# Gated state-space mix: sums of frequency products by accumulating transfers, product scratch by plane, unit matrix made on GpSimd, one new instruction order

## The chip, the core and the metric

The kernel runs on one core of a Trainium2 chip. The metric is the device time of one execution in microseconds (us), as the median of the runs shown. A profiled execution has a time of its own, and a span, which runs from its first instruction to its last.

## What is computed

There are L = 2048 tokens of D = 512 channels in bf16, x = A_u. Cut to what matters:

```python
K = einsum("dn,dnl,dn->dl", C, exp(dt*A*l), dt*B).real   # 128 complex states per channel, l = 0..2047
a = causal_convolution(x, K) + x * Dskip                 # the reference does it with FFTs of 4096
r = x @ w_r;  idx = the two tokens with the largest r
b = x;  b[idx] += (silu(x[idx] @ w_gate) * (x[idx] @ w_up)) @ w_down * sigmoid(r[idx])
g = sigmoid((x * gate_w).sum(-1))
out = g * a + (1 - g) * b
```

## The kernel before, in words

The 2048 tokens are two blocks of 1024 (`m` for inputs, `j` for outputs), and the 512 channels two halves of 256 (`c`, called `hf` in the early parts). The parts in the order of the program text:

- **Lead-in.** The tables of the state matrices are turned by matrix products with a unit matrix (`nt0`, `nt1`, L572), which VectorE (DVE) then combines with `dt`. The unit matrix and its negative (`CI`, 128x256) come by a transfer named `cia` from a constant (L525), which ScalarE (ACT) issues behind the transfer of `log_dt`. GpSimd (POOL) only fills a matrix of ones (`one`, L532). TensorE (PE) runs warm-up products `hm` on the ones (L535) until the data are there.
- **`transform(m)`**: the forward transform of a block, PE products (L870) evacuated by ACT or DVE (`fwo`, `fwe`), then DVE sums `v0`, `v1`, `w0`, `w1`. Two sums of each block are made by a transfer that adds its source into its destination (`vb`, `accum_op`, 512 KB, issued by POOL, L881 and L883).
- **Powers of the states**: exponentials on ACT (L437), DVE products `cm`, `mw`, `mf`, and for each half `coarse` and `fine` (PE phase sums at L681 and L686, sines on ACT, DVE products `pi`, `pr`, `qm`).
- **`lags(c)`**: PE sums over the states (`kmm`, L923), evacuations `kae`, a PE rearrangement `sel` (L937), evacuations `kce`, `kcx`. **`spectrum(c)`**: PE products `ks` (L962) and `kf` (L967), evacuated as `khe`, `khf`: the kernel's spectrum of this half.
- **`products(c, j)`** (L988): products of the token spectra with the kernel's. For j = 0 there are two DVE products (`prod`, 4096 wide), for j = 1 four for each half of the frequencies (2048 wide; `HALVES`, two stages `s_`). They then have to be summed: near block plus far block (j = 1 only), real parts (`yr`: first minus second), imaginary parts (`yi`: first plus second), and then sums and differences of the two frequency groups `hc` (`pq`), and for three of the four (c, j) another level (`b0`, `b2`, `b13`).
- **`inverse(c, j)`** (L1080): for each residue r of four, PE products with the inverse matrix (L1114), plus the residual `(1-g)/g * b` by a scaled unit matrix (L1109; `rd` makes that matrix), plus a correction (L1111), evacuated with the factor g (`ive`; ACT L1125 in two instructions, DVE L1129 in one), and sent out (`out`).
- **`rows`**: the gates, the choice of the two tokens and their feed-forward net: many tiny instructions on all engines, in the middle of the rest.

The product scratch lies in region TP. A product `k` has, for each frequency tile, 256 real and 256 imaginary columns in turn; `yr`, `yi` read runs of 256 columns (`pl_`, L1010). Before, the sums are made in one of two ways, chosen by `SUMPE` (L229): on DVE (`acc`, `yr`, `yi`, `pq`; used for (0, 0), (1, 0) and the first stage of (0, 1)), or on PE, which adds the products in PSUM with the unit matrix and its negative (`ac`, L1030, L1032, L1034), evacuated twice (`ace`) and followed by one `pq` (used for the second stage of (0, 1) and both stages of (1, 1)).

What sets the order: the program text only makes a list of operations with their buffers. `PLAN` (L180) is a written-out order of all of them, with a number for each that picks one of the engines that the operation may run on. Each engine runs its own operations in just that order, and waits with semaphores for what an operation needs (`replay` L128, `emit_plan` L152), also where the earlier operation ran on the same engine (PE excepted). SP, ACT and POOL issue transfers in that order too: a transfer that waits holds everything behind it on its issuing engine. `BANKS` (L215) gives the PSUM banks.

Nearly all DVE work is recorded at the lines of helpers: L408 (`tensor_tensor`), L434 (evacuations), L706 (`ns`), L859 (`fwo`), L1129 (`ive`), L1159 (`rd`); ACT's at L428 (copies and evacuations) and L437 (functions).

Of the kernel before, what the change touches and what calls it, by code (L numbers as in the profile page):

```python
# [179 lines left out]
PLAN = [(0, 0), (4, 0), (5, 0), (6, 0), (7, 0), (8, 0), (9, 0), (10, 0), (11, 0), (12, 0), (13, 0), (14, 0), (3, 0), (27, 0), (1, 1), (48, 0),  # L180
# [45 lines left out]
T2 = NEAR + [258, 262, 260, 264] + [516, 520, 772, 776] + [1032, 1544, 1288, 1800]  # L226
NT2 = 20
NG = 4
SUMPE = {(0, 0): False, (0, 1): (False, True), (1, 0): False, (1, 1): True}  # L229
QUARTER = {(0, 0): True, (0, 1): True, (1, 0): True, (1, 1): False}  # L230
MAGIC = 1.5 * 2.0 ** 39
TURN = 65536.0 / (2.0 * math.pi)
# [1008 lines left out]
```

## Time and profile before

| | |
|---|---|
| runs shown | 147.87, 149.94, 150.06 us; median 149.94 us |
| the profiled execution's own time | 148.18 us |
| its span | 146.4 us, mean granted TensorE clock 0.987 |
| busy | DVE 135.5 us (93%), PE 128.3 (88%), ACT 114.5 (78%), POOL 18.1 (12%) |
| transfers | 26.46 MB, mean 181 GB/s |

How to read it: times count from the start of the span. A group of instructions has its count behind "x", then the time that at least one of them was busy, then the mean of one in nanoseconds, then the idle time ahead of them with what ended it. Instructions of DVE start a little before the one ahead of them has ended, so the busy time of a group divided by its count is less than the mean of one. The chain that ended last is followed back from the last instruction. A line can be a helper's, and stand for many parts of the kernel.

### The profile page before, as it was taken

The numbers are of one execution on the slowest core, as the hardware profiler recorded it, in microseconds if no ns is written. First come the engines' busy times: TensorE is split into PE (matmuls) and PEld (weight loads), VectorE is DVE, ScalarE is ACT, GpSimd is POOL, SyncE is SP. The second block draws the span as 40 slices with busy tenths as digits, with TensorE's granted clock in tenths as the row PEclk, the third lists the DMA queues.
The fourth block names the chain that finished last, engine by engine and source line by source line (L and its number), as shares of the span: only waits on it lengthen the run. The fifth ranks groups of instructions, "written<-read, shape, count | busy, mean of one in ns | idle before, by whom it ended". The sixth has DMA issues, their size and how long they took to land.

```text
span 146.4 us, 3151 instructions
## 1 busy us (share of the span) xinstructions
PE 128.3 (88%) x1302; PEld 89.0 (61%) x1309; DVE 135.5 (93%) x174; ACT 114.5 (78%) x162; POOL 18.1 (12%) x30
## 2 busy tenths in 40 slices
PE   7956719999999979999979998888999898999992
PEld 3842306654434656566735886865888676778881
DVE  0699999989999999999999999999999999999962
ACT  3699999799999989699957878998499734517731
POOL 2000000180304804145310000000000000000000
PEclk9999999689999999999999999999999999999999
DMA  4779999899970809989646693735380050001345
GB/s 135 248 242 236 278 271 258 317 356 321 297 169 0 143 6 318 468 311 285 129 145 177 148 425 158 203 72 222 21 288 0 0 146 4 0 0 40 107 138 150
DMA packets 23741, 26.46 MB, mean 181 GB/s; under 512 B 9224, under 2 KB 20112, under 8 KB 23568
## 3 DMA queue, kind: packets, MB, share of 16 engines
q1 hardware_dynamic: 21134, 23.46, 52.4%
q0 software_dynamic: 1088, 2.10, 7.9%
q10 hardware_dynamic: 1506, 0.72, 1.7%
q8 instruction: 10, 0.16, 0.5%
q14 instruction: 3, 0.02, 0.0%
HBM read 19.85 MB, written 4.20 MB: 164 GB/s over the span
## 4 chain that ended last, share of the span: by engine, by line
DVE 44%; PE 33%; ACT 18%; issue 3%; POOL 0%; DVEq 0%; POOLq 0%
DVE RB L408 36%; ACT RB L437 11%; PE psm L1114 10%; ACT RB L428 6%; PE psm L962 5%; PE psm L1030 4%; DVE RB L434 3%; PE psm L1109 2%; PE psm L937 2%; PE psm L1034 2%; PE psm L1032 2%; DVE RB L706 2%; PE psm L535 2%; PE psm L681 1%; ACT L1186 1%
## 5 line engine op out<-in xcount | busy, mean ns | idle before, releaser
L408 DVE TENSOR_TENSOR RB<-RB 128x2048 bf16<-128x2048 bf16 (+8 forms) x120 | 113.0, 987 | 1.4 <-ACT RB L437 0.2
L428 ACT ACTIVATE RB<-psm 128x1024 bf16<-128x1024 f32 (+7 forms) x44 | 38.1, 898 | 15.4 <-PE psm L1034 9.2
L437 ACT ACTIVATE RB<-psm 128x1024 bf16<-128x1024 int16 (+1 forms) x37 | 36.5, 1033 | 6.4 <-PE psm L686 2.8
L1114 PE MATMUL psm<-RB 128*128 128x256 bf16 x160 | 22.3, 273 | 0.0
L681 PE MATMUL psm<-RB 128*128 128x256 f16 (+1 forms) x112 | 21.1, 336 | 0.2 <-ACT RB L428 0.2
L870 PE MATMUL psm<-RB 128*128 128x512 bf16 x61 | 15.0, 383 | 5.8 <-ACT RB L428 3.8
L437 ACT ACTIVATE RB<-RB 128x512 bf16<-128x512 f32 (+5 forms) x32 | 16.7, 591 | 1.3 <-DVE RB L408 1.2
L1114 PEld LDWEIGHTS psm<-RB 128*128 128x128 bf16 x160 | 15.7, 98 | 1.8
L686 PE MATMUL psm<-RB 128*128 128x512 f16 x44 | 13.5, 393 | 2.8 <-ACT RB L437 2.8
L962 PE MATMUL psm<-RB 128*128 128x256 bf16 x128 | 15.1, 273 | 0.8 <-ACT RB L428 0.8
L681 PEld LDWEIGHTS psm<-RB 128*128 128x128 f16 x112 | 10.8, 101 | 8.0 <-issue 0.5
L870 PEld LDWEIGHTS psm<-RB 128*128 128x128 bf16 x64 | 6.0, 100 | 14.5 <-ACT RB L428 4.7
L962 PEld LDWEIGHTS psm<-RB 128*128 128x128 bf16 x128 | 12.3, 98 | 3.4 <-ACT RB L428 1.6
L1125 ACT ACTIVATE RB<-psm,RB 128x256 bf16<-128x256 f32 x25 | 10.2, 472 | 5.2 <-PE psm L1114 4.2
L923 PE MATMUL psm<-RB 128*128 128x80 bf16 x256 | 10.4, 198 | 0.5 <-ACT RB L428 0.4
L923 PEld LDWEIGHTS psm<-RB 128*128 128x128 bf16 x256 | 9.7, 96 | 1.7 <-ACT RB L428 1.0
L1109 PE MATMUL psm<-RB 128*128 128x256 bf16 x32 | 8.7, 273 | 0.6 <-DVE RB L408 0.4
L428 ACT ACTIVATE RB<-psm,RB 128x1024 bf16<-128x1024 f32 (+1 forms) x9 | 9.2, 1062 | 0.0
L686 PEld LDWEIGHTS psm<-RB 128*128 128x128 f16 x44 | 3.5, 100 | 6.7 <-ACT RB L437 5.9
L1030 PE MATMUL psm<-RB 128*128 128x512 bf16 x21 | 6.5, 380 | 0.8 <-ACT RB L428 0.6
L883 POOL DMA_DIRECT2D RB<-RB x2 | 2.6, 1321 | 32.6 <-ACT RB L428 32.6
L434 DVE CAST RB<-psm 128x1024 bf16<-128x1024 f32 (+3 forms) x6 | 6.4, 1062 | 0.0
(71 smaller groups left out, 119.7 us busy)
## 6 DMA issues: line engine op xcount, KB each, us to landing
RB<-in_A_u_dram SPq DMA_DIRECT2D x8, 256.0 KB, 4.4
RB<-RB POOLq DMA_DIRECT2D x4, 512.0 KB, 9.8
RB<-c_near SPq DMA_DIRECT2D x4, 512.0 KB, 6.5
RB<-c_inv SPq DMA_DIRECT2D x1, 2048.0 KB, 10.4
RB<-u_routed SPq DMA_DIRECT2D x2, 1024.0 KB, 5.4
RB<-in_B_w_gate_dram SPq DMA_DIRECT2D x1, 1792.0 KB, 9.4
RB<-in_B_w_up_dram SPq DMA_DIRECT2D x1, 1792.0 KB, 16.8
RB<-in_B_w_down_dram SPq DMA_DIRECT2D x1, 1792.0 KB, 7.5
```

The lines of the kernel that those rows point to most:

```text
L408: return P.add(name, [(eng, c_dve(n, mode) if eng == DVE else 1.0, lambda h: h.tensor_tensor(out=o(), in0=a_(), in1=b_(), op=op))], rd, wr ...
L428: return lambda h: h.activation(out=o(), in_=a_(), func=ACTF.Copy, scale=scale() if callable(scale) else scale)
L434: return P.add(name, [(ACT, c_act(n), f_act(o, a_)), (DVE, c_dve(n, 1), lambda h: h.tensor_copy(o(), a_()))], rd, wr, **kw)
L437: return P.add(name, [(ACT, cost or c_act(n), lambda h: h.activation(out=o(), in_=a_(), func=func, scale=scale))], rd, wr, table=table, **kw)
L681: r = h.matmul(P32(t, 0, 0, 128, 256 * l0, (1, 256 * nl)), DGM(0, 128, (DD.index(d) + 2) * 128, (1, 128)), src(0, 128, col + hf * CW, (0, ...
L686: r = h.matmul(P32(t, b, 0, 128, 0, (1, 512)), DGM(0, 128, 0, (1, 128)), DGM(0, 128, 128 + c_, (0, 512)), start=False, stop=False, skip_gr ...
L870: x = h.matmul(P32(t, b, 0, 128, 0, (1, 512)), FM(0, 128, 2048 * par + 1024 * pl + 512 * i + 256 * q + 128 * b, (1, 128)), U(0, 128, ((m * ...
L923: x = h.matmul(P32(t, q // 6, 0, 128, (q % 6) * 80, (1, 80)), TPv(0, 128, ri * 16384 + c * 8192 + r * 128, (1, 128)), TQv(0, 128, c * 1024 ...
L962: x = h.matmul(P32(t, kt // 2, 0, 128, (kt % 2) * 256, (1, 256)), KN(0, 128, 2048 * KNP[2 * pl + hc] + 512 * g + 128 * kt, (1, 128)), KC[c ...
L1030: r = h.matmul(P32(t, kt, 0, 128, 0, (1, 512)), CI(0, 128, 0, (1, 128)), f(k, 0, 512), start=(k == 0 and hc == 1), stop=False, skip_group_ ...
L1109: h.matmul(o, RD(0, 128, (tb + 8) % 16 * 128, (1, 128)), UE[q](0, 128, r * 256, (1, 256)) if early else U2(0, 128, tb * D + c * CW, (1, 25 ...
L1114: x = h.matmul(o, G(0, 128, (pl * 4 + kt) * 1024 + (r * 2 + q) * 128, (1, 128)), PQ(0, 128, r * 1024 + kt * 256 + pl * 256 if quarter else ...
```

## The change

1. **Unit matrix.** The transfer `cia` goes. POOL makes `one`, then clears `CI` (`id0`) and writes the diagonals 1 and -1 with two `affine_select` over 128x128 each (`id1`, `id2`).
2. **Summing for c = 0.** `SUMPE` no longer names the second stage of (0, 1): its two `ac` on PE, two `ace` on ACT and one `pq` go, and it gets `yr` and two `pq` on DVE. In both stages of (0, 1) the two `acc` of DVE become one accumulating transfer `acd` of 1 MB that adds near and far products (all four planes). In (0, 0), both stages of (0, 1), and (1, 0) the `yi` of DVE becomes an accumulating transfer `yid` (512, 256, 256 and 512 KB). All six are issued by POOL. `yid` of a stage reads what `acd` of that stage has written.
3. **Planes.** A product summed by DVE or by transfer has all real columns first and then all imaginary ones (the write of `prod` and the reads of `pq` are stepped, `yr` reads whole runs). The second stage of (0, 1) gets scratch of its own (offset 16384 of TP, the first half of the second half-channel powers that `kmm` of `lags(1)` reads). The second stage of (1, 1) gets the region of the near matrix.
4. **Engines allowed.** `rs`, `rf`, `sel`, `mask`, `bu` may run on POOL too; the new plan puts `rs`, `sel`, `mask` there and `rf` on ACT.
5. **Order.** `PLAN` and `BANKS` are new throughout. Of the operations that both kernels have, these change engine. From DVE to ACT: `k0e`, `rf`, the first `rd`, and a net two evacuations `ive` of (1, 0) and one of (1, 1). From ACT to DVE: net one `fwo`, one `khe` (spectrum 0), one `kae` (lags 1), `z0`, one `ace` of (1, 1), two `ive` of (1, 1) and one of (0, 1). The order at the ends of the queues, where the numbers in round brackets are (c, j) and s0, s1 the stages:
   - DVE: two `khe` with `bu` between them, the last `qm` of `fine(1)`, 2 `prod`(0,0), `kae`, 4 `prod`(0,1)s1, `yr`(0,0), `pq`, `ku`, `b0`, `b2`, `pq`, 2 `b13`, 4 `prod`(0,1)s0, `ku`, `prod`(1,1)s1, `yr`(0,1)s1, then 3 `prod`(1,1), `pq`(0,1)s1, `prod`(1,1), 2 `b13`, `pq`, `prod`(1,1), `b2`, `b0`, 2 `prod`(1,1)s0, `yr`(0,1)s0, `prod`(1,0), `ace`(1,1), `pq`(0,1)s0, `b2`, `pq`, `b0`, 2 `b13`, `prod`(1,0), `ive`(1,1) r0, `pq`(1,1)s0, `ive`(0,1), `ive`(1,1) r2, `yr`(1,0), `pq`(1,1)s1, `pq`(1,0), `b2`, `pq`, `b0`, 2 `b13`, `ive`(1,0) r3.
   - PE: `kmm` and `sel` of lags 1, spectrum 1 with the four units of `inverse(0,0)` among it, the four `ac` of (1,1) (s1, s1, s0, s0), then all of `inverse(0,1)` and `inverse(1,1)` mixed (the second stage of (1,1) r2 is the tenth of them), then `inverse(1,0)` in the order r2, r0, r1, r3.
   - POOL: `yid`(0,0), `rr`, `acd`(0,1)s1, `yid` s1, `acd` s0, `yid` s0, `yid`(1,0).
   - SP: `out`(0,0), `out`(1,1) r0, the second load `u2` (1 MB), the other `out`.
   - ACT: `ace`(1,1), `rd` of the second block (eight instructions), `ace`(1,1), two `ive`(0,0), `ace`(1,1), `ive`.

The core of the diff:

```diff
-SUMPE = {(0, 0): False, (0, 1): (False, True), (1, 0): False, (1, 1): True}
+SUMPE = {(0, 0): False, (0, 1): False, (1, 0): False, (1, 1): True}
...
-        DMA("cia", lambda h: [h.dma_start(CI(0, 128, 0, (1, 256)), dr(id_c, 0, (640, 128), (1, 256)))], [], [bCIA], 64, rate=200.0, also=(ACT,))
+        P.add("one", [(POOL, 0.25, lambda h: h.memset(ONE(0, 128, 0, (1, 128)), 1.0))], [], [bONE])
+        P.add("id0", [(POOL, 0.25, lambda h: h.memset(CI(0, 128, 0, (1, 256)), 0.0))], [], [bCIA])
+        P.add("id1", [(POOL, 0.35, lambda h: h.affine_select(out=CI(0, 128, 0, (1, 128)), in_=CI(0, 128, 0, (1, 128)), compare_op=ALU.not_equal, fill=1.0, base=0, pattern=[[-1, 128]], channel_multiplier=1))], [bCIA], [bCIA])
+        P.add("id2", [(POOL, 0.35, lambda h: h.affine_select(out=CI(0, 128, 128, (1, 128)), in_=CI(0, 128, 128, (1, 128)), compare_op=ALU.not_equal, fill=-1.0, base=0, pattern=[[-1, 128]], channel_multiplier=1))], [bCIA], [bCIA])
...
+        PROB = {(0, 0): (32768,), (0, 1): (32768, 16384), (1, 0): (32768,), (1, 1): (16384, -16384)}
...
-                PRO = [(16384 if (c, j) == (1, 1) else 32768) + 2048 * nk * k for k in range(4 if j else 2)]
+                PRO = [PROB[c, j][s_] + 2048 * nk * k for k in range(4 if j else 2)]
...
-                    TT("prod", lambda: PR[k](0, 128, 0, (1, 1024 * nk)), vin, kk, ALU.mult, ...
+                    TT("prod", (lambda: PR[k](0, 128, 0, (256, 2 * nk), (512 * nk, 2), (1, 256))) if plane else lambda: PR[k](0, 128, 0, (1, 1024 * nk)), vin, kk, ALU.mult, ...
...
                     if j == 1:
-                        for k in range(2):
-                            TT("acc", ...
+                        if (c, s_) in ((0, 0), (0, 1)):
+                            pr_ = lambda k, nk=nk, PRO=PRO: at("TP", PRO[k], 4096 * nk, BF)(0, 128, 0, (1024 * nk, 2), (1, 1024 * nk))
+                            DMA("acd", lambda h, pr_=pr_: [h.dma_start(pr_(0), pr_(2), accum_op=ALU.add, max_dma_last_dim=2048)], [x for y in bP for x in y], bP[0] + bP[1], 1024, eng=POOL, issue=1.3, lat=3.8, rate=155.0)
...
-                    TT("yr", pl_(0, 0), pl_(0, 0), pl_(1, 1), ALU.subtract, [bP[0][0], bP[1][1]], [bP[0][0]], 512 * nk)
-                    TT("yi", pl_(0, 1), pl_(0, 1), pl_(1, 0), ALU.add, [bP[0][1], bP[1][0]], [bP[0][1]], 512 * nk)
+                    pn = lambda k, pl, PR=PR, nk=nk: (lambda: PR[k](0, 128, pl * 512 * nk, (1, 512 * nk)))
+                    TT("yr", pn(0, 0), pn(0, 0), pn(1, 1), ALU.subtract, [bP[0][0], bP[1][1]], [bP[0][0]], 512 * nk)
+                    if (c, j, s_) in ((0, 0, 0), (0, 1, 0), (0, 1, 1), (1, 0, 0)):
+                        DMA("yid", lambda h, pn=pn: [h.dma_start(pn(0, 1)(), pn(1, 0)(), accum_op=ALU.add, max_dma_last_dim=2048)], [bP[0][1], bP[1][0]], [bP[0][1]], 128 * nk, eng=POOL, issue=1.3, lat=3.8, rate=155.0)
+                    else:
+                        TT("yi", pn(0, 1), pn(0, 1), pn(1, 0), ALU.add, [bP[0][1], bP[1][0]], [bP[0][1]], 512 * nk)
```

More of the change, by code (lines that the diff above doesn't have):

```diff
@@ L368, in bass_gated_mix__ssm_conv_s4__moe_arch_mod__prompt_kernel @@
         sems = {e: es.enter_context(nc.semaphore("s_" + e)) for e in ENGS}
-        dsem = [es.enter_context(nc.semaphore("d%d" % i)) for i in range(64)]
+        dsem = [es.enter_context(nc.semaphore("d%d" % i)) for i in range(80)]
         block = es.enter_context(nc.Block())
@@ L531, in bass_gated_mix__ssm_conv_s4__moe_arch_mod__prompt_kernel @@
         row = lambda v, c=0, n=D: (lambda: v(0, 128, c, (1, n)))
-        P.add("one", [(POOL, 0.3, lambda h: h.memset(ONE(0, 128, 0, (1, 128)), 1.0))], [], [bONE])
         twm = P.pst(1, "hm")
@@ L779, in bass_gated_mix__ssm_conv_s4__moe_arch_mod__prompt_kernel @@
             if c == 0:
-                TS("sel", row(cand, 0, 16), idx, one1(v), ALU.is_equal, [bRT[v], bCF], [bcand], 16, s2=-3.0e38, op1=ALU.mult)
-                TT("mask", row(rb2, 0, 16), row(cand, 0, 16), row(rb2, 0, 16), ALU.add, [bcand, brb2], [brb2], 16, 1)
+                also_pool(TS("sel", row(cand, 0, 16), idx, one1(v), ALU.is_equal, [bRT[v], bCF], [bcand], 16, s2=-3.0e38, op1=ALU.mult))
+                also_pool(TT("mask", row(rb2, 0, 16), row(cand, 0, 16), row(rb2, 0, 16), ALU.add, [bcand, brb2], [brb2], 16, 1))
         TT("rs0", one1("rs0"), one1("m1"), lambda: CF(0, 128, 144, (1, 1)), ALU.mult, [bRT["m1"], bCF], [bRT["rs0"]], 1, 1, eng=POOL)
@@ L1000, in part, with prod @@
                                                                    for kt in kts_ for hc in hcs for pl in pls])
-                def prod(k, m, i, pl, k0_=k0_, nk=nk, PR=PR, bufs=None):
+                def prod(k, m, i, pl, k0_=k0_, nk=nk, PR=PR, bufs=None, plane=False):
                     if nk == 4 and m == 1:
@@ L1006, in prod @@
                     kk = lambda: KH[c](0, 128, i * 4096 + k0_ * 1024 + pl * 256, (512, 2 * nk), (0, 2), (1, 256))
-                    TT("prod", lambda: PR[k](0, 128, 0, (1, 1024 * nk)), vin, kk, ALU.mult, [x for y in bV[m] for x in y] + [bKH[c][i][hc][pl] for hc in range(2)], bufs, 1024 * nk)
+                    TT("prod", (lambda: PR[k](0, 128, 0, (256, 2 * nk), (512 * nk, 2), (1, 256))) if plane else lambda: PR[k](0, 128, 0, (1, 1024 * nk)), vin, kk, ALU.mult, [x for y in bV[m] for x in y] + [bKH[c][i][hc][pl] for hc in range(2)], bufs, 1024 * nk)
                 pl_ = lambda k, pl, PR=PR, nk=nk: (lambda: PR[k](0, 128, pl * 256, (512, 2 * nk), (1, 256)))
@@ L1045, in products @@
                 else:
-                    bP = [[part("pr%d" % pl, k, (0, 1), (pl,)) for pl in range(2)] for k in range(4 if j else 2)]
+                    bP = [[P.buf("pr%d%d%d%d_%d" % (pl, c, j, k, s_), [("sb", base["TP"] + PRO[k] + 1024 * nk * pl, base["TP"] + PRO[k] + 1024 * nk * (pl + 1))]) for pl in range(2)] for k in range(4 if j else 2)]
                     for k, m, i, pl in ks:
-                        prod(k, m, i, pl, bufs=bP[k])
+                        prod(k, m, i, pl, bufs=bP[k], plane=True)
```

22 lines of the change are left out of this document (14 added, 8 removed), and 68 rows, old and new, of the table PLAN.

## The prediction

> **What bounds the kernel now.** I read the page first, then busy times by stretch, then DVE's order of time at the end.
>
> ```profile
> span 146.4 us, 3151 instructions
> PE 128.3 (88%) x1302; PEld 89.0 (61%) x1309; DVE 135.5 (93%) x174; ACT 114.5 (78%) x162; POOL 18.1 (12%) x30
> ```
> ```profile
> core 0: us, PE busy (x) PEld busy (x) DVE busy (x) ACT busy (x) POOL busy (x), PEclk, DMA share, GB/s
> 20.00:45.00 25.00, 22.46 (x158) 12.07 (x161) 24.25 (x46) 24.00 (x30) 5.34 (x8) 0.93 0.94 271
> ...
> 66.00:90.00 24.00, 22.11 (x270) 15.82 (x267) 23.93 (x29) 18.82 (x22) 3.66 (x8) 1.00 0.73 220
> 90.00:110.00 20.00, 18.27 (x270) 14.98 (x269) 19.66 (x21) 17.39 (x28) 0.00 (x0) 1.00 0.54 151
> 110.00:130.00 20.00, 19.04 (x151) 14.22 (x151) 19.83 (x24) 11.15 (x15) 0.00 (x0) 1.00 0.10 27
> 130.00:140.00 10.00, 9.95 (x91) 8.74 (x90) 9.90 (x10) 6.57 (x15) 0.00 (x0) 1.00 0.19 54
> ```
> ```profile
> 88.71 51.41 DVE L408 TENSOR_TENSOR RB<-RB 128x2048 bf16<-128x2048 bf16 x55
> ...
> 143.56 0.42 DVE L1129 TENSOR_TENSOR RB<-psm,RB 128x256 bf16<-128x256 f32 x1 [0.18 <-PE psm L1114]
> ```
>
> DVE is the bound nearly everywhere: 24.25 of 25, 23.93 of 24, and from 88.71 (the last `qm` of `fine(1)`) 55 instructions without a break to 140.12. PE is a second bound behind 110 (19.04 of 20, 9.95 of 10) and ends the run: DVE's last four instructions wait for inverse products. So a gain must shorten DVE's list, and PE's queue must not take its place.
>
> **DVE's work.** The prices, as busy time over count:
>
> ```profile
> L408 DVE TENSOR_TENSOR RB<-RB 128x2048 bf16<-128x2048 bf16 x60 | 71.3, 1218 | 0.7
> L408 DVE TENSOR_TENSOR RB<-RB 128x1024 bf16<-128x1024 bf16 x31 | 20.5, 686 | 0.2
> L408 DVE TENSOR_TENSOR RB<-RB 128x4096 bf16<-128x4096 bf16 x4 | 9.1, 2281 | 0.0
> L408 DVE TENSOR_TENSOR RB<-RB 128x512 bf16<-128x512 bf16 x8 | 3.0, 421 | 0.2
> L434 DVE CAST RB<-psm 128x1024 bf16<-128x1024 f32 x2 | 2.4, 1212 | 0.0
> L1129 DVE TENSOR_TENSOR RB<-psm,RB 128x512 bf16<-128x512 f32 x3 | 2.1, 692 | 1.2 <-PE psm L1114 1.2
> L1159 DVE TENSOR_TENSOR RB<-RB 128x1024 bf16<-128x1024 bf16 x1 | 1.2, 1206 | 0.0
> L434 DVE CAST RB<-psm 32x512 bf16<-32x512 f32 x1 | 0.7, 698 | 0.0
> ```
>
> That is 1.19 for 2048 columns, 0.66 for 1024, 2.28 for 4096, 0.38 for 512, 1.2 for an evacuation of 1024, 0.7 for an `ive`. Gone from DVE: two `yi` and two `acc` of 2048 (4.76), a `yi` and a `pq` of 1024 (1.32), `k0e` 0.7, `rd` 1.2, `rf`, `sel`, `mask` (16 columns wide, some 0.2 each), two whole `ive` and a half one (1.8): 10.4. Added: `yr` and two `pq` (1.98), `fwo`, `khe`, `ace` (3.6), `kae` (960 columns) 1.15, three `ive` 2.1, `z0` 0.15: 9.0. Net -1.4: most of what the transfers take from DVE is filled again. And of the `ive`, four (2.5) now run behind the last `b13`, where DVE waits anyway; in the new order one (0.7) does. Up to the last `b13` DVE's work is +0.4 (-1.4+2.5-0.7). I price the plane layout at nothing: `prod` writes and `pq` reads runs of 256 columns in steps, as `yr`, `yi` do in these rows at the same 1.19. The dear end would be `rd`'s row, twice the price for 1024 columns, but its second operand repeats one element; here every operand stays in runs of 256, which excludes that end.
>
> The new order does save something, where an instruction no longer reads the one directly ahead:
>
> ```profile
> 43.83 1.24 DVE RB L408
> ...
> 45.09 4.51 DVE RB L408 x4
> ```
> Here the next instruction (a `pr` behind its `pi`) starts 1.26 behind; the four that follow take 1.13 each. I count 0.1 for such a pair. The plan before has 32, the new one about 20: -1.2, of which -0.7 ahead of the last `qm`.
>
> **Lead-in.**
>
> ```profile
> 0.72 0.20 POOL L532 MEMSET RB<- 128x128 bf16 x1 [0.29 <-POOLq L1226]
> 3.23 0.10 PEld L539 LDWEIGHTS psm<-RB 1*128 1x128 bf16 x1 [0.41 <-issue]
> 3.77 1.41 PEld L572 LDWEIGHTS psm<-RB 128*128 128x128 bf16 x8 [0.44 <-DMA RB<-c_id]
> 3.87 0.60 ACT L437 ACTIVATE RB<-psm 128x512 bf16<-128x512 f32 x1 [1.86 <-PE psm L539]
> 4.91 0.69 DVE L408 TENSOR_TENSOR RB<-RB,psm 128x512 f32<-128x512 bf16 x1 [4.91 <-PE psm L572]
> ```
> ```profile
> 28.70 1.38 POOL L883 DMA_DIRECT2D RB<-RB  x1 [27.31 <-ACT RB L428]
> 29.68 0.83 POOL L422 CAST RB<-RB 128x16 bf16<-128x16 f32 x1
> 29.88 1.81 POOL L881 DMA_DIRECT2D RB<-RB  x1
> 32.05 0.46 POOL L412 TENSOR_SCALAR RB<-RB 128x16 f32<-128x16 f32 x1 [0.37 <-ACT RB L437]
> ```
> The turn of the tables waits 0.44 for the unit matrix, and DVE starts at 4.91. On POOL the matrix is ready at 0.92, plus a clearing, plus two `affine_select`, which the trace does not have: the nearest rows are POOL's, from 0.20 (the clearing's kind) to 0.83, so 0.6 to 2.5 for the three. That gives 1.5 to 3.4, against 3.33, where PE is free. The gain ends at 4.47, where ACT's `dt` is done: 0 to -0.4, I take -0.3. On POOL `e0` moves back by as much; nothing reads it before DVE's `cm`. The loads of the lead-in change order too (the transposed `xt` goes ahead of half of the first block). I price that at nothing, because DVE's and ACT's full lists (24.25 and 24.00 of 25) cover a later load; without that cover DVE stands idle at `fwo` by as much as the load is late.
>
> **The place of the last `qm`.** Gone ahead of it: a `prod` of (0,0) (2.28), `rd`, `k0e` and the small ones (2.5); added: `fwo` and `khe` (2.4) and `z0`. So it starts at 88.71-2.2-0.7-0.3 = 85.5 and ends at 86.7. From there DVE's list to the last `prod` of (1,1) has 2 of 4096 columns, 19 of 2048, 7 of 1024, 4 of 512, a `kae` and two small `ku` (some 0.3): 35.1. The same counting gives 52.5 for the 55 instructions that took 51.41, so I scale by 0.98: 34.4, end 121.1. The second-stage scratch adds a wait: the four `prod`(0,1)s1 may only write when `kmm` of lags 1 has read there.
>
> ```profile
> 90.92 3.83 PE L923 MATMUL psm<-RB 128*128 128x80 bf16 x96
> 95.14 1.32 PE L923 MATMUL psm<-RB 128*128 128x80 bf16 x32 [0.39 <-ACT RB L428]
> ```
> `kmm` takes 5.5 (90.92 to 96.46); from 86.7 it ends at about 92.4, just when DVE has done two `prod` and `kae` (5.7). Between 0 and 1; I take 0.3: 121.4.
>
> **PE's queue behind it.** The two `ac` of PE that go save work, but the order puts all of `inverse(0,1)`, `(1,1)` and `(1,0)` behind the last `ac`(1,1).
>
> ```profile
> 119.59 0.43 PE psm L1030 x2
> 120.02 0.22 PE psm L1032 x2
> 120.24 0.22 PE psm L1034 x2
> ...
> 131.23 3.49 PE psm L1114 x32
> ```
> ```profile
> L428 ACT ACTIVATE RB<-psm 128x1024 bf16<-128x1024 f32 x26 | 26.4, 1036 | 13.2 <-PE psm L1034 9.2 <-PE psm L962 3.9
> ```
> An `ac` is twice these three rows, 1.74. The two of stage s0 share a PSUM tile, so behind 121.4 stand `ac`, `ace` 1.04, `ac`, with three handovers of 0.1: 126.2. Then 44+76+42 = 162 matmuls of 256 columns at 0.109 (3.49 over 32): 17.7, and 0.3 of waiting for `b2` of (0,1): 144.2. Behind the last comes an `ive` (0.69), a handover (0.15), and what lies between the last `ive` before (143.98) and the end, 2.4: **147.5, +1.1**.
>
> DVE's own way: from 121.4 its list to the second `prod`(1,0) is 9.1 (130.5); `ive`, `pq`, `ive` to 132.6; the next `ive` needs the tenth inverse unit, 72 matmuls behind 126.2, 134.0: a wait of 1.4; with `ive`, `yr`, `pq` 136.7; then `pq`, `b2`, `pq`, `b0`, 2 `b13` (5.0) to 141.7; units r1 and r3 (21 matmuls, 2.3) and the same 3.25: 147.3. Both ways end together.
>
> **The transfers.**
>
> ```profile
> q0 software_dynamic: 1088, 2.10, 7.9%
> ```
> ```profile
> DMA to landing us min/median/max: 8.5/9.8/11.1
> ```
> ```profile
> DMA to landing us min/median/max: 5.1/9.8/14.5
> ```
> These are the four accumulating transfers, 512 KB each (L883, then L881). 7.9% of 146.4 is 11.6 of all engines, 2.9 each; the 5.1 was alone, so 2.2 is fixed. That gives 3.7 for 256 KB and 8.0 for 1 MB (bounds: 5.1, and 15.7 for the first two together, from 28.70 to 29.88+14.5). Cover on DVE: `yid`(0,0) 7.1 (`kae`, 4 `prod`, `yr`), against 5.1; `acd` s1 12.7, with its `yid` 16.9, against 11.7; `acd` s0 13.3, with `yid` 17.5; `yid`(1,0) 4.6 plus the wait of 1.4, 6.0, against 5.1. All covered in the likeliest case, the last by least: without that wait it costs 0.5, and at 8.5, beside the second `u2`, which SP issues in those microseconds, 2.5.
>
> **Sum.** 146.4 + 1.1 = 147.5; the profiled execution's own 148.18 lies 1.76 below the median of the runs, so I add the difference to the median: 149.94 + 1.1 = **151.0 us**.
>
> **Rivals.**
> - *PE's queue does not take over* (0.24). If the `ac` come some 1.5 earlier and DVE does not wait for the tenth unit, DVE's way is left: 147.3-1.4 = 145.9, and 0.7 less if more pairs part: 145.2, **148.7 us**. For it: DVE's work falls by 1.4 in all and PE's by 3.5. Against: 162 matmuls behind one point of DVE's list.
> - *ACT holds the last `ac`* (0.14), slower. `rd` lies between the first and second `ace`(1,1) on ACT, eight instructions.
> ```profile
> L1157 ACT ACTIVATE RB<-RB 128x128 bf16<-128x128 bf16 x8 | 2.5, 388 | 0.0
> ```
>   If ACT is so far behind that this falls into the chain of `ac`, 2.5 are added: 150.0, **153.5 us**. It decides once the first `ace` ends later than about 120.5; I place it at 120.2.
> - *The 1 MB transfers land late* (0.12), slower. The `yid` of s1 waits for the first `acd` and holds the second on POOL's queue. At 15.7 the first, issued at 97.1, lands at 112.8, the second, issued 1.2 behind, at 129.7, and `yr` of s0 waits for it from 121.4: +8, **159 us**. It decides from 11.5 on; at 12.5 2% is passed. Against it: DMA share 0.54 and 0.10 in those stretches, 0.94 where the 14.5 was. The Trainium skill's page "DMA: Bandwidth & Descriptors" (Anatomy of one DMA) fits 2.0 us plus bytes over 436e3, an estimate of 3.2 for 512 KB; the trace's 5.1 is slower, and by that rule this rival would vanish.
> - *The unit matrix comes late* (0.04), slower. The rows ahead of POOL's first `TENSOR_SCALAR` bound what a first use can hide: 28.70 to 32.05, 3.35. Put ahead of the selects, it gives 5.4 instead of 3.77, +1.6, **152.6 us**. The Trainium skill's "GPSIMD Engine Reference" (2.1 Instruction dispatch) has about 6 us for the first call of a freshly loaded kernel; that would be +4. Against it speaks the idle 0.37 ahead of the first `TENSOR_SCALAR`, which ended with ACT.
>
> **How the numbers follow.** The forecast's own case has 0.46. Its own range is 149 to 153. The first rival and the spread of the runs reach down to 147.4, the slower ones up to 154.4; outside lie the late transfers and part of the fastest cases, together under 2 in 10. 2% of 149.94 is 3.0, about what a measurement of this kernel tells from no change: faster than 146.9 is 0.07 (a part of the first rival), slower than 152.9 is 0.25 (most of the slower rivals, the top of the forecast's case), within it 0.68.
>
> **What would show it.** Right: DVE busy near 134; first DVE instruction near 4.6; the `kmm` of lags 1 from about 87; the L1030 group down to two thirds and ending about 126, with PE unbroken from there to the end; the last `b13` at 141 to 142; 1 MB landing in 7 to 10. Wrong: PE idle behind 126 with DVE still unbroken (first rival), DVE waiting for a transfer (third), `ac` apart by more than 3 (second), or DVE starting behind 5 (fourth).

## The result, and the profile after

The changed kernel takes 160.6 us (median of 4 runs, 159.1 to 160.9) against 148.9 us before (147.8 to 150.1, same chip): 1.0805 times as long, 95% interval 1.0749 to 1.0861. The forecast was 151.0, with a range of 147.4 to 154.4. The profiled execution of the changed kernel took 159.07 us with a span of 157.3; the forecast's sum had a span of 147.5. The runs of one kernel differ with the clock that TensorE is granted (159.1 us at a mean of 0.957, 160.9 at 0.925), so the times below are medians of all runs of a kernel, and the ratios to the kernel before leave out, on both sides, the runs that lie more than 1.5% above the fastest of theirs.

From the page of the changed kernel: the span, busy times, the clock in tenths over 40 slices, and the chain that ended last.

```profile
span 157.3 us, 3120 instructions
...
PE 128.0 (81%) x1280; PEld 88.6 (56%) x1285; DVE 133.4 (85%) x171; ACT 110.6 (70%) x163; POOL 36.4 (23%) x42
...
PEclk9995977999999999999999999999559999999999
...
PE 34%; DVE 26%; ACT 22%; DMA 12%; issue 3%; SPq 1%; POOL 0%; ACTq 0%; POOLq 0%
```

VectorE's work came out as counted (133.4, forecast "near 134"). Its share fell from 93% to 85%, so it stood idle. The chain now holds 12% of transfers. Busy times in the stretches used in the prediction, with its columns (PE, PEld, DVE, ACT, POOL; then TensorE's clock, DMA share and GB/s), show where:

```profile
20.00:45.00 25.00, 22.56 (x141) 12.05 (x141) 24.09 (x42) 24.08 (x30) 11.88 (x12) 0.93 0.89 275
66.00:90.00 24.00, 22.54 (x276) 16.27 (x273) 23.16 (x27) 18.83 (x23) 1.03 (x2) 1.00 0.78 224
90.00:110.00 20.00, 13.13 (x215) 10.71 (x211) 19.09 (x19) 14.05 (x22) 2.74 (x3) 1.00 0.83 194
110.00:130.00 20.00, 13.76 (x93) 10.13 (x94) 12.85 (x17) 8.44 (x16) 3.07 (x3) 0.83 0.47 81
```

In 110 to 130 VectorE works 12.85 of 20 us (19.83 before), and TensorE had already idled 7 of 20 us in the stretch ahead (13.13, 18.27 before). What VectorE waited for (us in total, times, longest):

```profile
DVE RB L408 <- ACT RB L433: 7.1, 2, 6.8
DVE RB L1145 <- PE psm L1130: 5.0, 3, 2.7
...
DVE RB L408 <- DMA RB<-RB: 0.4, 1, 0.4
```

One wait of 6.8 us, for an evacuation by ScalarE; and only 0.4 for the new transfers. The orders of time of five engines around that wait (start, duration, then in brackets the idle time ahead and what ended it), VectorE first:

```profile
119.46 4.10 DVE L408 TENSOR_TENSOR RB<-RB 128x2048 bf16<-128x2048 bf16 x4 [6.83 <-ACT RB L433]
```
```profile
118.32 1.11 ACT L433 ACTIVATE RB<-psm,RB 128x1024 bf16<-128x1024 f32 x1 [9.02 <-PE psm L974]
```
```profile
106.16 0.60 PE L974 MATMUL psm<-RB 128*128 128x256 bf16 x4
112.53 0.40 PE L1125 MATMUL psm<-RB 128*128 128x256 bf16 x1 [5.77 <-DMA RB<-u_routed]
...
114.64 1.06 PE L974 MATMUL psm<-RB 128*128 128x256 bf16 x4
```
```profile
97.25 0.51 SPq L1162 DMA_DIRECT2D RB<-c_tail  x1
100.87 1.20 SPq L955 DMA_DIRECT2D RB<-RB  x2
102.11 4.20 SPq L1168 DMA_DIRECT2D RB<-u_routed  x1
```
```profile
100.07 1.30 POOL L1060 DMA_DIRECT2D RB<-RB  x1 [5.17 <-DVE RB L408]
112.21 0.87 POOL L1067 DMA_DIRECT2D RB<-RB  x1 [10.85 <-DMA RB<-RB]
```

Read from the bottom. At 100.07 POOL issues the first 1 MB accumulating transfer (`acd` of stage s1). SP has been free since 97.76, but its next entry is `kt` of lags 1 (L955), which waits for that part's evacuations until 100.87. Only behind it stands the second `ue` (L1168), 256 KB of routed tokens for `inverse(0,0)`: issued at 102.11, and then beside the 1 MB transfer. TensorE has four units of `inverse(0,0)` (L1125) among the sums `ks`, `kf` (L969, L974) of spectrum 1, and since it runs its list in order it stands at the first of them for 5.77 us, until the load lands. The `kf` of spectrum 1 that was next comes at 114.64 instead of about 107, ScalarE evacuates the last of what the waiting product reads at 118.32 (9.02 idle), and VectorE's product of (1,1) starts at 119.46. In the chain of the changed kernel the load is one row (the second row is the late `u2`, of which more below):

```profile
102.11 10.37 DMA RB<-u_routed
...
141.33 7.74 DMA RB<-u_routed
```

So a load that the diff does not touch, other than by its place in the order, took 10.4 us to land and held three engines in turn. What this does not say is which of its causes counts: its late issue, the traffic beside it, or TensorE's order.

### The profile page after: what moved, and what is told of

Same layout as the page of the kernel before. It is cut to its first block, busy times and chain, and to the rows that moved or that the text cites. A ratio compares the mean times of both kernels' runs of the same rounds, so it can differ in the third digit from the quotient of the medians.

```text
span 157.3 us, 3120 instructions
## 1 busy us (share of the span) xinstructions
PE 128.0 (81%) x1280; PEld 88.6 (56%) x1285; DVE 133.4 (85%) x171; ACT 110.6 (70%) x163; POOL 36.4 (23%) x42
## 3 DMA queue, kind: packets, MB, share of 16 engines
q0 software_dynamic: 2976, 5.77, 21.8%
## 4 chain that ended last, share of the span: by engine, by line
PE 34%; DVE 26%; ACT 22%; DMA 12%; issue 3%; SPq 1%; POOL 0%; ACTq 0%; POOLq 0%
DVE RB L408 20%; DMA RB<-u_routed 12%; ACT RB L442 11%; ACT RB L433 11%; PE psm L1130 6%; PE psm L688 5%; PE psm L969 4%; PE psm L944 3%; PE psm L930 3%; PE psm L693 3%; PE psm L877 2%; PE psm L1125 2%; PE psm L542 2%; DVE RB L439 1%; PE psm L974 1%
## 5 line engine op out<-in xcount | busy, mean ns | idle before, releaser
L408 DVE TENSOR_TENSOR RB<-RB 128x2048 bf16<-128x2048 bf16 (+10 forms) x116 | 108.6, 983 | 8.2 <-ACT RB L433 7.1
L433 ACT ACTIVATE RB<-psm 128x1024 bf16<-128x1024 f32 (+7 forms) x38 | 33.0, 887 | 11.7 <-PE psm L1042 5.1
L1130 PE MATMUL psm<-RB 128*128 128x256 bf16 x160 | 23.6, 286 | 0.0
L1067 POOL DMA_DIRECT2D RB<-RB x4 | 4.2, 1039 | 61.6 <-DVE RB L408 43.6
L877 PE MATMUL psm<-RB 128*128 128x512 bf16 x61 | 16.3, 405 | 2.0 <-DVE RB L866 1.3
L1130 PEld LDWEIGHTS psm<-RB 128*128 128x128 bf16 x160 | 16.5, 103 | 2.5
L1141 ACT ACTIVATE RB<-psm,RB 128x256 bf16<-128x256 f32 x24 | 9.3, 485 | 11.1 <-PE psm L1130 11.1
L969 PE MATMUL psm<-RB 128*128 128x256 bf16 x128 | 15.0, 273 | 2.0 <-ACT RB L433 2.0
L688 PEld LDWEIGHTS psm<-RB 128*128 128x128 f16 x112 | 10.6, 101 | 8.8 <-ACT RB L442 1.8
L969 PEld LDWEIGHTS psm<-RB 128*128 128x128 bf16 x128 | 12.4, 98 | 4.5 <-ACT RB L433 2.6
L1125 PE MATMUL psm<-RB 128*128 128x256 bf16 x32 | 9.3, 291 | 6.3 <-DMA RB<-u_routed 6.2
L877 PEld LDWEIGHTS psm<-RB 128*128 128x128 bf16 x64 | 6.3, 103 | 10.2 <-DVE RB L866 2.1
L930 PEld LDWEIGHTS psm<-RB 128*128 128x128 bf16 x256 | 10.1, 96 | 2.4 <-ACT RB L433 0.8
L930 PE MATMUL psm<-RB 128*128 128x80 bf16 x256 | 10.8, 198 | 0.7 <-ACT RB L433 0.7
L439 DVE CAST RB<-psm 128x1024 bf16<-128x1024 f32 (+2 forms) x8 | 9.3, 1160 | 1.4 <-PE psm L930 0.8
L414 POOL TENSOR_SCALAR RB<-RB 128x16 f32<-128x16 f32 (+3 forms) x6 | 9.2, 1533 | 3.9 <-DVE RB L777 3.6
L1038 PE MATMUL psm<-RB 128*128 128x512 bf16 x15 | 4.6, 381 | 5.2 <-DVE RB L408 2.9
## 6 DMA issues: line engine op xcount, KB each, us to landing
RB<-in_B_w_gate_dram SPq DMA_DIRECT2D x1, 1792.0 KB, 10.4
```

The lines of the kernel that those rows point to most:

```text
L408: return P.add(name, [(eng, c_dve(n, mode) if eng == DVE else 1.0, lambda h: h.tensor_tensor(out=o(), in0=a_(), in1=b_(), op=op))], rd, wr ...
L433: return lambda h: h.activation(out=o(), in_=a_(), func=ACTF.Copy, scale=scale() if callable(scale) else scale)
L439: return P.add(name, [(ACT, c_act(n), f_act(o, a_)), (DVE, c_dve(n, 1), lambda h: h.tensor_copy(o(), a_()))], rd, wr, **kw)
L688: r = h.matmul(P32(t, 0, 0, 128, 256 * l0, (1, 256 * nl)), DGM(0, 128, (DD.index(d) + 2) * 128, (1, 128)), src(0, 128, col + hf * CW, (0, ...
L877: x = h.matmul(P32(t, b, 0, 128, 0, (1, 512)), FM(0, 128, 2048 * par + 1024 * pl + 512 * i + 256 * q + 128 * b, (1, 128)), U(0, 128, ((m * ...
L930: x = h.matmul(P32(t, q // 6, 0, 128, (q % 6) * 80, (1, 80)), TPv(0, 128, ri * 16384 + c * 8192 + r * 128, (1, 128)), TQv(0, 128, c * 1024 ...
```

## The experiments

All are edits of the changed kernel. **The load's place, or its reader's.** Two kernels take away one link each:

```diff
 PLAN (second ue early)
-(341, 0), (372, 0), ... (439, 0), (340, 0), (486, 0)
+(341, 0), (340, 0), (372, 0), ... (439, 0), (486, 0)
 PLAN (inverse (0,0) late)
-(381, 0), (494, 0), (384, 0), ... (383, 0), (498, 0), (382, 0)
+(494, 0), ... (498, 0), (381, 0), (384, 0), (383, 0), (382, 0)
```

> One entry of the order is moved: the second 256 KB load `ue` of routed tokens is issued by SP right behind the first one, ahead of `u8`, `u2`, `tm` and of `kt` of the second half. In the changed kernel SP stood at `kt` (issued 100.87 and 101.49) and issued this load at 102.11; it landed at 112.5, the first matmul of inverse (0,0) started at 112.53, and VectorE's first product of (1,1) came 6.83 us late, at 119.46. Theory (SP's order of issue): the load leaves at about 96, lands by 103, inverse (0,0) starts when ScalarE has turned the rows `rd` (106.2), the 6.83 us gap falls under 1 us, TensorE's clock does not drop, and the time falls by 6 to 7.5 us to 153 to 154.5. Rival (the accumulating transfers take the bandwidth): the load lands late whatever its place, after 108, and the time stays above 156.5. Rival (inverse (0,0) only reveals a ScalarE that is overloaded): the gap moves to another releaser on ScalarE and the time stays above 158.

> TensorE's four groups of inverse (0,0) are moved behind the last matmul of the second half's spectrum; the loads keep their places. Theory (the late load reaches VectorE only because TensorE holds inverse (0,0) ahead of the spectrum's sums): the sums `kf` and `ks` run from about 106.2 on, ScalarE has evacuated them by about 111, the 6.83 us gap ahead of the first product of (1,1) falls under 1 us although the load still lands at about 112, and the time falls by 6 to 7.5 us to 153 to 154.5. Rival (ScalarE itself is what is late): the gap stays above 4 us and the time above 158. Rival (the clock drop of TensorE is the cause of the loss): TensorE still idles for several us around 110, the drop stays, and the time falls by under 3 us.

With the load early: 154.0 us (one run of 151.0 at a mean clock of 0.989, three of 153.8 to 154.4 at 0.933 to 0.944; before on that chip 147.9). Both loads leave together, and the gap is gone:

```profile
92.56 1.30 SPq L1167 DMA_DIRECT2D RB<-u_routed  x2
...
102.55 1.24 SPq L954 DMA_DIRECT2D RB<-RB  x2
```
```profile
DVE RB L1144 <- PE psm L1129: 5.8, 3, 2.6
...
DVE RB L407 <- ACT RB L432: 0.5, 2, 0.3
```

With the reader late: 153.0 us (151.7 to 157.3; ratio to before 1.0301, interval 1.0204 to 1.0399), although the load still took as long (then two of VectorE's waits):

```profile
RB<-u_routed SPq DMA_DIRECT2D x1, 256.0 KB, 10.5
```
```profile
DVE RB L407 <- ACT RB L432: 2.0, 2, 1.7
...
DVE RB L407 <- PE psm L968: 1.0, 1, 1.0
```

Both medians came in as the theories had them (153 to 154.5). The profiled execution of the second kernel, though, is its slowest (157.28 us): the wait of 6.8 us is gone there, but waits of 1.7 and 1.0 us are left, where under 1 us was expected. A measure that leaves out what lies ahead is the time from the last `qm` to the last `ive` on VectorE: 66.5 us in the changed kernel (87.53 to 153.99), 60.1 with the load early (89.19 to 149.26), 62.8 with the reader late (89.25 to 152.07). So late load and TensorE's order are each a link without which the long wait does not happen, the first worth all of it in its profile, the second somewhat more than half. The rivals (an overloaded ScalarE, a load that is late wherever it stands) fall.

The clock has a part, as a consequence of the wait. It drops in TensorE's idle stretch (0.50 from 111 on), so from the first matmul behind it to the third group of `kf` TensorE takes 5.2 us (112.53 to 117.68), and 2.8 in the kernel below that has one of the sums on VectorE (107.83 to 110.59): some 2.4 us of VectorE's lateness are half clock. In the second kernel the clock dropped as well (0.82 in 110 to 115, 0.83 in 115 to 120), with the waits that are left.

**The traffic beside it.** One kernel makes all six accumulating transfers VectorE instructions, one only the 1 MB transfer of s1 (the first two lines of the diff, for s1 alone); the load stays late in both.

```diff
-DMA("acd", lambda h, pr_=pr_: [h.dma_start(pr_(0), pr_(2), accum_op=ALU.add, ...)], ...)
+TT("acd", lambda: pr_(0), lambda: pr_(0), lambda: pr_(2), ALU.add, ..., 2048 * nk)
-if (c, j, s_) in ((0, 0, 0), (0, 1, 0), (0, 1, 1), (1, 0, 0)):   # yid
+if False:
```

> The six accumulating transfers become VectorE instructions at the same places of the order: two sums of 128x4096 and four of 128x2048 or 128x1024; everything else of the changed kernel stays, the late load too. VectorE gets about 8 us of work more, 4.0 of them ahead of the 6.83 us gap and 4.0 behind it. Theory (SP's order): the load `ue` is still issued at about 102; without the 1 MB transfer beside it, it lands earlier, at about 106.5 (the two `ue` loads took 3.8 us in the kernel before), so that the gap closes: 160.6 - 6.8 + 8.0 = 161.8. If contention had no part in its 10.4 us it lands at 112 as before, the gap takes up the first 4.0, and the time is 164.6. Rival (the transfers themselves are what makes the kernel slow, through their landing or their contention elsewhere): the time falls clearly, under 157.

> Of the six accumulating transfers of the changed kernel only one goes to VectorE, the 1 MB sum of the second half of (0,1) that was issued at 100.07 and held the DMA engines from 101.94 to 111.58; the second `ue` stays late, behind `kt`. VectorE gets 2.2 us more, ahead of the gap. Theory (that one transfer, beside it on the DMA engines, stretched the landing of `ue` from 4.3 us, as with all six gone, to 10.4): the load lands at about 106.5, the 6.83 us gap is under 1 us, and the time is 160.6 - 6.8 + 2.2 = 156. Rival (the transfer of 512 KB ahead of it, or the 1 MB `u2`, stretched it): the load still takes over 8 us, the gap takes up the 2.2 and the time stays at 160 to 161.

Landing times of the load, and of the smaller `kt` ahead of it (KB each, median us), around 100 us: the changed kernel, then all six gone, then the one (with the 1 MB transfer that is left there).

```profile
RB<-u_routed SPq DMA_DIRECT2D x1, 256.0 KB, 10.4
...
RB<-RB SPq DMA_DIRECT2D x1, 16.0 KB, 8.6
```
```profile
RB<-u_routed SPq DMA_DIRECT2D x1, 256.0 KB, 4.3
...
RB<-RB SPq DMA_DIRECT2D x1, 16.0 KB, 3.4
```
```profile
RB<-RB POOLq DMA_DIRECT2D x1, 1024.0 KB, 7.9
RB<-u_routed SPq DMA_DIRECT2D x1, 256.0 KB, 4.4
```

The one 1 MB transfer made 10.4 of 4.4 (SP's issue of the load alone took 4.20 us beside it, 1.54 and 1.71 without); the 1 MB transfer that is left, of s0, lands in 7.9. In the run with the one sum on VectorE the load is issued as late (101.69), lands by 106.1 and holds nobody: it takes the late issue and the traffic together. That kernel's time is 155.6 us (1.0435, 1.0314 to 1.0556; 156 expected): 1.9 us more VectorE work (135.3 against 133.4), and still 5.0 us faster than the changed kernel. With all six on VectorE it is 161.0 (161.8 expected): the gap is closed, and VectorE's 7.5 us more (140.9 busy against 133.4) fill it. So in this order the transfers took 7.5 us off VectorE and gave as much back as one wait. That they do save work, once nothing on the path stands beside them, shows in the next kernel, with the load early and all six on VectorE:

> The second `ue` early, and the six accumulating transfers as VectorE instructions at the same places, so that the transfers are priced without the 6.83 us gap that swallowed VectorE's work before. VectorE gets about 8.0 us more, 4.0 ahead of the last products of (1,1) and 4.0 behind. Theory (with the late load out of the way VectorE sets the start of TensorE's last stretch again): the first 4.0 us show in full and up to 2 of the others, 4 to 6 us above the run with `ue` early, 158 to 160. Rival (the transfers give back in waits and contention what they take off VectorE): within 1.5 us of the run with `ue` early.

162.3 us (159.9 to 163.3; 1.0781, 1.0696 to 1.0866), 8.3 above the kernel with the load early alone. The forecast of 4 to 6 was too low: the whole of VectorE's 7.6 us (141.1 busy against 133.5) shows from the last `qm` to the last `ive`, 67.7 us against 60.1, with the same clock of 0.77 in 10 to 40 ahead of it in both profiles.

**The second `u2`.** SP issues it at 141 behind its outputs, and the chain goes through its landing (141.33 and 7.74, so 149.07). Moved behind `kt` (entry 440 behind 438), once without and once with the fillings below:

> As the run with the second `ue` early, and the second `u2` (1 MB, in the changed kernel issued at 141 behind SP's outputs, landed at 149.07, with the first matmul of the last stretch at 149.21) is issued right behind `kt` of the second half as well. Theory (the late load holds TensorE's last stretch): the idle time of TensorE ahead of its last 40 matmuls goes, and the time is 1 to 2 us below the run with `ue` alone, 151.5 to 153. Rival (the last butterflies of (1,0), done at 151.3, would hold the end anyway): within 0.5 us of the run with `ue` alone.

> All of that, and the second `u2` issued right behind `kt` of the second half as well. In the run with `u2` early the last stretch of TensorE ended 17.8 us after its start as in the others, so u2 had been hidden. Theory (TensorE's queue of the last stretch sets the end): within 0.5 us of the run with both fillings. Rival (the late `u2` holds the end as soon as the stretch starts earlier): 0.8 to 1.5 us below it.

153.6 and 152.5 us, against 154.0 and 152.2 without: no difference. Already in the changed kernel TensorE stood only 0.4 us for it. A wait that stands in the chain need not be one that costs.

**VectorE's waits for evacuations.** Four `PLAN` entries with the other engine (427, 480, 550, 554 from 1 to 0):

> The second `ue` early, and four evacuations of PSUM that the new order gave to VectorE go to ScalarE at the same places (`kae` of the second half, and three `ive` of the last stretch). In the run with `ue` early VectorE stood 0.84 us ahead of the first and 1.2 and 1.9 us ahead of two of the others, waiting for TensorE, with the last sums of (1,0) queued behind. Theory (these waits of an in-order VectorE hold the last butterflies): they go, with 3.2 us of work, the last butterfly comes 4 to 6 us earlier and the time falls by 2 to 3 us. Rival (TensorE's queue of the last stretch, unbroken from 131, sets the end): the last butterfly comes earlier, the time stays within 0.8 us of the run with `ue` early.

153.9 us (1.0307, 1.0238 to 1.0376): the rival is right. VectorE had less to do and spent it waiting, for the `yid` of (1,0) and then for the last inverse product:

```profile
DVE RB L1144 <- PE psm L1129: 4.2, 1, 4.2
DVE RB L407 <- DMA RB<-RB: 3.5, 1, 3.5
```

**The clock.** Matmuls that nobody reads, put where TensorE idles:

```diff
+for n in (9, 17, 20):  fill(n)     # n matmuls CI x CI of 256 columns into a free bank
 PLAN
+(559, 0) behind (429, 0); (560, 0) behind (433, 0); (561, 0) behind (388, 0)
 second kernel also
+16 behind (54, 0); 24 behind (187, 0)
```

> The second `ue` early, and 46 matmuls of the unit matrix with itself that nobody reads, 9 ahead of and 17 behind the lags' selection of the second half (where TensorE idles 1.1 and 2.0 us), and 20 behind inverse (0,0) (2.4 us idle). In the run with `ue` early the granted clock was 0.79 and 0.87 in 100 to 110 and 0.67 in 120 to 125, and 48 spectrum matmuls took 7.08 us (5.42 in the changed kernel, at 1.00). Theory (idle stretches of 2 to 3 us let the clock drop, and the drop costs about 1.7 us at the spectrum and 1.7 at the first `ac` group): the clock is 1.00 in both places, the 48 matmuls take 5.5 us, and the time falls by 2 to 3.4 us, to 150.7 to 152. Rival (the drop lies under VectorE's work): the clock is restored but the time moves by under 0.8 us. Rival (idle time is not what drops the clock): the clock stays low there and the time rises by up to 1 us.

> As the run with the second `ue` early and the 46 filling matmuls, and 40 more of them early: 16 behind the weights' turn (TensorE idle from about 9.6 to 11.5) and 24 behind the first two groups of the transform (idle from 13.5 to 16.2). In the run without these the clock was granted at 0.50 from about 17 to 30 and at 1.00 from 38 to the end; VectorE worked 8.8 and 9.05 of the 10 us in 20 to 30 and 30 to 40 (9.94 and 9.38 in the kernel before), and the time was 153.9 in all five runs. Theory (the early half clock delays the transform and the polar form, so VectorE, which bounds this part, stands): the clock stays at 1.00 in 12 to 36, VectorE's share there is back above 9.3, the last `qm` of (1) starts 1.5 to 2.5 us earlier than its 88.7, and the time is 151 to 152.4, as the one run with `ue` early at a mean clock of 0.989 had (151.0). Rival (VectorE and ScalarE make up for it behind): the clock is restored, the time stays above 153.2.

Stretches of the kernel with the load early, then of the one with the first fillings, then with all:

```profile
20.00:40.00 20.00, 18.70 (x101) 9.67 (x98) 17.46 (x34) 17.75 (x23) 9.09 (x10) 0.72 0.83 293
100.00:110.00 10.00, 7.97 (x65) 6.04 (x54) 9.93 (x13) 5.55 (x13) 1.30 (x1) 0.83 0.99 229
```
```profile
20.00:40.00 20.00, 18.06 (x103) 9.49 (x103) 17.87 (x35) 18.21 (x24) 10.02 (x10) 0.74 0.85 294
100.00:110.00 10.00, 9.95 (x93) 8.60 (x90) 9.93 (x12) 7.61 (x15) 1.30 (x1) 1.00 0.98 226
```
```profile
20.00:40.00 20.00, 17.85 (x134) 9.98 (x135) 18.69 (x35) 18.82 (x25) 9.26 (x10) 0.91 0.93 317
100.00:110.00 10.00, 9.95 (x92) 8.55 (x90) 9.93 (x13) 7.50 (x14) 1.30 (x1) 1.00 0.91 209
```

In the middle the clock went from 0.83 to 1.00 and the time stayed (153.9, 1.035, 1.0299 to 1.0402): VectorE was as busy (9.93 of 10) at either clock. My theory for that place was wrong. Early, where VectorE waits for TensorE's turns and transforms (17.9 of 20 us), 0.74 to 0.91 brought 0.8 us of VectorE's time within this stretch, and 1.7 us in all: 152.2 us (1.0229, 1.0179 to 1.028). Of the 11.7 us lost, then, some 6.4 are the load (66.5 against 60.1 behind the last `qm`), and up to some 1.7 an early half clock, of which the profiled executions have more or less: in 10 to 40 the clock was 0.94 in the kernel before, 0.89 in the changed one, 0.77 with the load early and 0.94 with all fillings.

**What is left.** One more kernel gives the products of the first stage of (1,1) another place in memory, so that the sums of the second stage of (0,1) may go behind them, and one moves `inverse(0,0)` too:

```diff
-(1, 1): (16384, -16384)}
+(1, 1): (0, -16384)}
 PLAN
-(460, 0), ... (463, 0), ... (467, 0), (466, 0), (462, 0), ... (465, 0), (464, 0), ... (523, 0)
+... (523, 0), (460, 0), (463, 0), (467, 0), (466, 0), (462, 0), (465, 0), (464, 0)
```

> The run with both fillings, and one change of memory: the products of the first stage of (1,1) are written over the half-0 spectra (dead by then) and no longer over the scratch of stage s1 of (0,1). So the last products of (1,1) need no longer wait for the sums of that stage, and the seven VectorE instructions of these sums (one `yr`, two `pq`, `b0`, `b2`, two `b13`: 3.1 us) go behind the last product of (1,1). Theory (what is left over the kernel before is TensorE's last stretch, some 23.5 us from the last product of (1,1) to the last matmul, so that it shifts with that product): the last product ends 2.5 to 3.1 us earlier, at about 120.6 to 121.2, the last matmul as much earlier, and the time is 149.1 to 149.9, within 1.5% of the kernel before. Rival (ScalarE's evacuations of the second half's spectrum hold the products as soon as they come earlier): the products gain under 1 us, 151.2 to 152. Rival (the sums, now later, hold TensorE's last stretch): the products come 2.5 us earlier, TensorE then idles, and the time falls by under 1 us.

> As the run with the new scratch place, and inverse (0,0) behind the second half's spectrum on TensorE. Theory (TensorE's last stretch): ScalarE has the spectrum out earlier, which helps only if it held the products: within 0.5 us of the run with the new scratch place where that run shows no wait of the products for ScalarE, and up to 1 us below it where it does. Rival (inverse (0,0), moved to the idle time of TensorE around 115, delays the first `ac`): 0.5 to 1.5 us above it.

154.4 us (1.0394, 1.0341 to 1.0447) and 155.3 (1.0347, 1.0281 to 1.0414): slower, not faster, and not faster at the same mean clock either (153.2 at 0.977, and 153.0 and 153.6 at 0.989, against 152.2 at 0.975 and 152.3 at 0.989 with all fillings). The profiled execution of the first lost time ahead of the edit: the last `qm` started 2.2 us later, in a part with the same instructions, at a mean clock of 0.967 against 0.989. Counted from the last `qm`, the rows of VectorE (last `qm`, the last two products of (1,1), last `ive`) of the kernel with all fillings, then of the one with the new place:

```profile
87.80 1.23 DVE L408 TENSOR_TENSOR RB<-RB 128x2048 bf16<-128x2048 bf16 x1 [0.16 <-ACT RB L442]
...
121.30 2.36 DVE L408 TENSOR_TENSOR RB<-RB 128x2048 bf16<-128x2048 bf16 x2
...
147.14 0.69 DVE L1145 TENSOR_TENSOR RB<-psm,RB 128x512 bf16<-128x512 f32 x1 [2.62 <-PE psm L1130]
```
```profile
90.00 1.23 DVE L408 TENSOR_TENSOR RB<-RB 128x2048 bf16<-128x2048 bf16 x1 [0.16 <-ACT RB L442]
...
120.39 2.35 DVE L408 TENSOR_TENSOR RB<-RB 128x2048 bf16<-128x2048 bf16 x2
...
149.70 0.69 DVE L1145 TENSOR_TENSOR RB<-psm,RB 128x512 bf16<-128x512 f32 x1 [2.56 <-PE psm L1130]
```
```profile
131.31 0.28 PE L1125 MATMUL psm<-RB 128*128 128x256 bf16 x1 [2.14 <-DVE RB L408]
```

From the last `qm` to the end of the last product: 35.9, then 32.7 us, 3.1 less, as meant. From there to the last `ive`: 23.5, then 27.0. All of it is given back, and TensorE's last stretch now waits 2.14 us for VectorE's sums, where the run with all fillings had none there (its waits for VectorE, 1.9 us, lie at the `ac` before it): the last rival. TensorE's queue and VectorE's list end together, and moving work along VectorE's list gained nothing here. In the second kernel the early clock was better (mean 0.978), but a product of (1,1) waited 2.2 us for ScalarE, so nothing came of it. No version here beats the kernel before; the nearest ratio is 1.0229, with all fillings.

## Why the prediction was wrong

- **The step that failed** is the one on the transfers: "All covered in the likeliest case". It priced them by when VectorE needs their results, and there it held: VectorE waited 0.4 us for them. It did not ask which other transfers are under way meanwhile, nor who waits for those. In its place the runs showed a load of 256 KB that landed in 10.4 us instead of 4.4 beside the first 1 MB transfer, issued 4.35 us behind the time at which SP was free, and through TensorE (5.77 us idle) and ScalarE a wait of 6.83 us on VectorE, at a place where the prediction has none. The `ue` loads are not in the prediction at all. SP's list was in reach (`kt` of lags 1 ahead of the second `ue`, free to issue from 97.76), and so was TensorE's (`inverse(0,0)` among spectrum 1); both lists only had to be walked with the question what each entry waits for.
- **The third rival** (a 1 MB transfer lands late, 159 us) came near the time by another mechanism. The transfer did take about 12 us (issued at 100.07; POOL's next entry, which waits for it, went at 112.21), over the 11.5 from which that rival was to decide, but the `yr` behind it had no wait. Nearness of a number is no evidence for its mechanism. The 8.0 that the forecast gave 1 MB is what one takes without neighbours (7.9 in the run with s1 on VectorE); beside the loads, which it slows, it was slowed itself, too.
- **The size of the 1 MB transfer's traffic.** In 90 to 110 the DMA engines were busy 0.83 of the time at 194 GB/s (0.54 and 151 before). The Trainium skill's page "DMA: Bandwidth & Descriptors" (section "Issuing engines are not separate DMA queues") says that transfers started by SP, ACT and GpSimd run on the same 16 engines and interleave; the load at 10.4 beside the transfer and at 4.4 without it agrees.
- **DVE's work** was right: 133.4 against "near 134". **Adjacent pairs** came about as counted (ahead of the last `qm` 21 instructions of VectorE start only behind the end of the one ahead, 27 in the kernel before), but the same order put new waits there that the prediction did not look for, and the last `qm` started at 87.53, not 85.5:

```profile
DVE RB L866 <- PE psm L877: 0.8, 2, 0.6
DVE RB L439 <- PE psm L944: 0.6, 1, 0.6
```
  With a share of 24.25 of 25 in 20 to 45 and 23.93 of 24 in 66 to 90 in the kernel before (24.09 and 23.16 now), VectorE "busy nearly everywhere" was read as a property of the stretch; it was a property of the old order.
- **Lead-in.** The matrix was ready in time, as forecast (an `affine_select` took 0.29 us, the last ended at 2.15), but VectorE started at 4.84 and not 4.6: TensorE's turn still began at 3.77, now behind the `dt` product. That product ran from 3.23 for 0.60 us in the kernel before too, so TensorE was not free at 3.33, as the prediction read it. The rival of a late unit matrix was wrong.
```profile
1.86 0.29 POOL L533 TENSOR_SCALAR_AFFINE_SELECT RB<-RB 128x128 bf16<-128x128 bf16 x1
...
3.77 1.56 PE L579 MATMUL psm<-RB 128*128 128x128 bf16 x8
...
4.84 0.69 DVE L408 TENSOR_TENSOR RB<-RB,psm 128x512 f32<-128x512 bf16 x1 [4.84 <-PE psm L579]
```
- **TensorE's queue at the end** was right in kind and size: 22.8 us forecast from the last product of (1,1) to the last matmul, 23.5 in the kernel with all fillings. That VectorE's own way ends at the same time (147.3 against 147.5) was right as well, as the moves by the last kernels show.
- **The sum.** The span was 9.8 us over the forecast: 6.8 for the gap, 2.0 up to the last `qm`, 0.5 for `kae` (0.84 waited, 0.3 forecast), 0.7 for the queue at the end, and -0.2 for the rest. The median moved further than the profiled execution, whose mean clock (0.957) was the highest of the four runs (0.925 to 0.935 in the others); in which part of those the clock was lower is not shown. Left open is how much of the 2.3% that remain belongs to each of these small terms; the kernels above do not part them.

## What to carry to other kernels

Moving work from an engine to a transfer does not make it free: look for the other transfers in its microseconds, and for who waits for those, before asking whether its own reader waits. In an order written out by hand, walk the list of each issuing queue and of the in-order engines, and ask of each entry what it waits for and what stands behind it; a small load behind a waiting entry can cost about as much as all the work that is moved saves (here 6.8 us against 7.5). When an experiment or a rival hits the number, check the mechanism in the trace too.

## What the runs showed that was not expected

- A 256 KB load landed in 4.4 us alone and in 10.4 beside a 1 MB accumulating transfer; a 16 KB copy in 3.4 and 8.6. An accumulating transfer moves slowly and still fills all 16 engines: the 1 MB transfer without neighbours moved 189 GB/s, with the engines busy throughout (114.5 to 119.5 of the kernel with one sum on VectorE).
- After an idle stretch of 5.77 us TensorE's clock was 0.57 in 110 to 115; the same four `kf` matmuls took 0.60 us at 106.16 and 1.06 at 114.64. Early, behind an idle stretch of 2.7 us, the kernel with the load early was held at 0.50 for 12 us, with TensorE busy for 10.8 of them (the changed kernel, then that one):
```profile
110.00:115.00 5.00, 2.47 (x12) 1.79 (x13) 2.60 (x4) 0.00 (x0) 2.18 (x2) 0.57 0.33 57
```
```profile
16.24 2.36 PE L876 MATMUL psm<-RB 128*128 128x512 bf16 x8 [2.70 <-DVE RB L865]
```
```profile
18.00:30.00 12.00, 10.82 (x89) 5.67 (x88) 10.80 (x21) 10.29 (x16) 1.76 (x3) 0.50 0.94 330
```
  The Trainium skill's "TensorE: Matmul & The Clock Gate" (Part 1) gives at least one window of about 3.4 us of sustained work to get the full clock back. Here it took some 5 us behind 112.53 (full from about 117.5), and in the early stretch more than the 12.
- A drop of the clock costs nothing where TensorE's result is not what ends last: restoring it from 0.83 to 1.00 at 100 to 110 left the time as it was.
